# Layer-norm statistics on ScalarE for five tiles, one transposed buffer for two layers, and a new order of loads and matmuls in an MLP-mixer block

## The chip, the cores and the metric

One core of a Trainium2 chip runs the kernel. The metric is the device time of one execution in microseconds. Its engines: PE (TensorE, the matmuls), DVE (VectorE), ACT (ScalarE), POOL (GpSimd), SP (SyncE, which here only issues DMAs). "PEld" is PE's loading of weights, which overlaps its matmuls.

## The reference

x has 2048 rows of 512 in bf16; w1 and w2 are 512x512, w3 is 512x1792, w4 is 1792x512.

```python
def _layernorm(x, axis=-1, eps=1e-5):
    m = jnp.mean(x, axis=axis, keepdims=True)
    v = jnp.var(x, axis=axis, keepdims=True)
    return (x - m) / jnp.sqrt(v + eps)

def reference(x, w1, w2, w3, w4):
    B, S, D = x.shape
    h = _gelu(_layernorm(x, axis=-1) @ w1)
    c = D // 4
    g0 = jnp.pad(h[:, :, 0*c:1*c], ((0, 0), (1, 0), (0, 0)))[:, :S, :]
    g1 = jnp.pad(h[:, :, 1*c:2*c], ((0, 0), (0, 1), (0, 0)))[:, 1:, :]
    g2 = jnp.pad(h[:, :, 2*c:3*c], ((0, 0), (2, 0), (0, 0)))[:, :S, :]
    g3 = jnp.pad(h[:, :, 3*c:   ], ((0, 0), (0, 2), (0, 0)))[:, 2:, :]
    hs = jnp.concatenate([g0, g1, g2, g3], axis=-1) @ w2
    x1 = x + hs
    h2 = _gelu(_layernorm(x1, axis=-1) @ w3) @ w4
    return x1 + h2
```

## The kernel before

The rows are cut into 16 tiles of 128. Tile t of layer 1 has the number q = t, of layer 2 the number q = 16 + t. All weights and all of x stay in SBUF; each is read once.

**Stages.** `ln` (L272) makes statistics and normalized rows of a tile: bn_stats (L275, "bnst"), bn_aggr (L277, "bnag"), then the inverse root. For tiles 0 and 1 that is a square root on ACT (L281) and a reciprocal on DVE (L283); for the rest variance plus epsilon on DVE (L287, "vpe") and a power of -0.5 on POOL (L290, "rstd"). The rows are normalized on DVE (L296), ACT (L304) or POOL (L307), by the table `NORM`; ACT and POOL also need "nmr" (L300), minus mean times rstd, from DVE. Matmuls need the tile transposed: by four PE transposes (`pe_transpose`, L316; matmul on L327, eviction on ACT L334 or DVE L337, by the table `EVAC`) for the tiles that the script names with `tp` or `ty` (they differ in the PSUM buffer), by a DMA transpose on SP (L313, "tp") for the rest.

`mm_up` (L341) multiplies the transposed rows of a group of tiles by w1 or w3 (L355), 128 output features at a time, and gelu on ACT (L370) evicts PSUM. `GROUPS` gives the tiles per group; a group of n tiles has matmuls of 128n columns. `mm_mix` (L379) multiplies the four shifted quarters of gelu's output by w2 for one tile (L395, four matmuls of 512 columns); shifts of one and two rows mean that it needs its neighbours' groups too. DVE adds x (L401, "x1"), and `ln(2, t)` follows. `mm_down` (L406) multiplies by w4 (L419, 14 matmuls of 512 columns, the last tile in two halves); DVE adds x1 (L427) and SP writes the tile out.

PSUM has three pairs of banks (`next_pair`) for up groups and `ty` transposes, and two single banks (`next_bank`) for mix, down and `tp` transposes; each is used in turn, so a step waits until the eviction of the step that held it last.

**Order.** PE follows `SCRIPT` exactly. A planner in `Program.order` (L48) lays out the other engines ahead of time: each operation has a cost and a due time counted back from PE's order, and the earliest due of the ready ones goes next. Every engine then runs its list strictly in that order, with semaphore waits where an operation needs another engine's result. An engine whose next operation isn't ready stands still, whatever is ready behind it. The loads go ahead of everything on SP. Twelve matmuls on zeros (L443) warm PE up. Two activations on a constant (L450, L452) bring in the tables for square root and gelu.

SP's order of loads before: x tiles 0, 1, 2, 3 (one each), w1 in two halves, x tiles 4-5, 6-7, w2, w3, x tiles 8-11, 12-15, w4 in two halves; then DMA transposes and writes.

The orders that the planner makes, of ACT and of PE, up to PE's first large stretch:

```
ACT  warm_sqrt sqrt1 sqrt0 warm_gelu ev1 ev0 ev2 gelu1_1 gelu1_0 gelu1_2 norm4 gelu1_3 norm7 ev4 ev6 gelu1_4 gelu1_5 gelu2_0 ...
PE   warm tp1 tp0 up1_1 tp2 up1_0 tp3 up1_2 mix0 tp5 up1_3 mix1 tp4 mix2 tp7 tp6 up1_4 up1_5 tp16 tp17 mix3 mix4 up2_0 ...
```

("up1_4" is group 4 of layer 1, "gelu1_4" its gelu, "ev" the eviction of a PE transpose.)

Of the kernel before, what the change touches and what calls it, by code (L numbers as in the profile page):

```python
# [6 lines left out]
P = 128  # L7
# [18 lines left out]
class Program:  # L26
# [17 lines left out]
    def line(self, names):  # L44

        self.lines.append(names.split())

    def order(self):  # L48
# [24 lines left out]
        named = {op.name: op for op in self.ops}  # L73
        for names in self.lines:
            for a, b in zip(names, names[1:]):
                assert named[a].eng == named[b].eng, (a, b)
                preds[named[b].idx].add(named[a].idx)
        last = None
        pe_pos = 0
        for op in self.ops:  # L80
            if op.eng == "pe":
                if last is not None:
                    preds[op.idx].add(last.idx)
                last = op
                op.prio = pe_pos
                pe_pos += 1
        succs = [set() for _ in self.ops]
# [41 lines left out]
        for op in self.ops:  # L129
            if op.first is not None:  # L130
                op.prio = op.first

# [8 lines left out]
        qfree = 0.0  # L141
        out = []
        while len(out) < len(self.ops):
# [12 lines left out]
            if op.queue is None:  # L156
                done = free[e] = start + op.dur
            else:
                free[e] = start + (1300.0 if op.queue == "tp" else (1000.0 if e == "pool" else 460.0))
                if op.queue == "tp":  # L160
                    done = max(start + 2300.0, qfree + 1200.0)
                else:
                    qfree = max(qfree, start + 1500.0) + op.dur
                    done = qfree + 350.0
            out.append(op)
            for j in succs[op.idx]:
# [3 lines left out]
                ready[j] = max(ready[j], done + hop)  # L170
                if npend[j] == 0:
                    cands[o.eng].append(o)
        self.seq = out
        self.total = max(free.values())
        return out

GROUPS = {1: (1, 1, 1, 1, 2, 2, 4, 4), 2: (2, 2, 4, 4, 4)}
NORM = {0: "pool", 4: "act", 5: "pool", 6: "pool", 7: "act", 8: "pool", 9: "pool", 10: "act", 11: "act", 16: "pool", 19: "pool", 20: "act", 21: "act"}
EVAC = {3: "dve", 5: "dve", 7: "dve", 16: "dve", 17: "dve"}
SCRIPT = """  # L180
warm:3 warm:9 ty:1 ty:0 up1:1 tp:2 up1:0 tp:3 up1:2 mix:0 ty:5 up1:3 mix:1 ty:4 mix:2 ty:7 ty:6 up1:4-5
ty:16-17 mix:3-4 up2:0 mix:5 up2:1 down:0 mix:6 up1:6 down:3 mix:7 mix:9-10 up1:7 mix:8 down:1 mix:14 up2:2
mix:15 mix:13 mix:11 down:7 down:2 down:6 down:5 mix:12 up2:3 down:4 down:11 down:10 up2:4 down:8 down:14
down:12 down:9 down:13 down:15
"""

def bass_standalone__mixer_s_mlp__prompt_kernel(nc, x, w1, w2, w3, w4, out):
# [5 lines left out]
    NHEAD = 2  # L193
    NXN, NO, NPAIR, NOB = 12, 4, 3, 2
    SHIFT = (1, -1, 2, -2)
    HTW = S + 4
    group_of = {(l, t): g for l in (1, 2) for g, (t0, n) in enumerate(groups[l]) for t in range(t0, t0 + n)}
# [4 lines left out]
    with ExitStack() as es:  # L202
# [4 lines left out]
        x1nT = sb("x1nT", [P, DC, S], BF16)  # L207
# [14 lines left out]
        sdv = sb("sdv", [P, NHEAD], F32)  # L222
# [10 lines left out]
        npair, nbank = [0], [0]  # L233
# [9 lines left out]
        def y_res(p):  # L243
            return [("y", p)]
# [16 lines left out]
        def load_x(eng, t0, n, after=()):  # L261
            return pg.add(eng, f"x_dma{t0}", lambda e: e.dma_start(x_sb[:, t0 : t0 + n, :], xt[:, t0 : t0 + n, :]),  # L262
                   reads=list(after), writes=[(("x", t), 0) for t in range(t0, t0 + n)], dur=n * 400.0, queue=eng)

        def load_w(eng, name, dst, src, c0, c1, after=()):
            return pg.add(eng, f"dma_{name}{c0}",
                   lambda e: e.dma_start(dst[:, c0:c1, :], src.rearrange("(c p) f -> p c f", p=P)[:, c0:c1, :]),  # L267
                   reads=list(after), writes=[((name, c), 0) for c in range(c0, c1)],
                   dur=(c1 - c0) * P * src.shape[1] * 2 / 330.0, queue=eng)


        def ln(layer, t):  # L272
            q = t if layer == 1 else NT + t
            src, rs = (x_sb[:, t, :], ("x", t)) if layer == 1 else (x1_sb[:, t, :], ("x1", t))
            pg.add("dve", f"bnst{q}", lambda e: e.bn_stats(st6[:, q, :], src),  # L275
                   reads=[(rs, 0)], writes=[(("st6", q), 0)], dur=605)
            pg.add("dve", f"bnag{q}", lambda e: e.bn_aggr(mv[:, q, :], st6[:, q, :]),  # L277
                   reads=[(("st6", q), 0)], writes=[(("mv", q), 0)], dur=75)
            if q < NHEAD:
                pg.add("act", f"sqrt{q}",  # L280
                       lambda e: e.activation(sdv[:, q : q + 1], mv[:, q, 1:2], ACT_F.Sqrt, bias=eps_c[:], scale=1.0),  # L281
                       reads=[(("mv", q), 0), (("eps",), 0), (("warm",), 0)], writes=[(("sdv", q), 0)], dur=190)
                pg.add("dve", f"rcp{q}", lambda e: e.reciprocal(rstd[:, q : q + 1], sdv[:, q : q + 1]),  # L283
                       reads=[(("sdv", q), 0)], writes=[(("rstd", q), 0)], dur=75)
            else:
                pg.add("dve", f"vpe{q}",
                       lambda e: e.tensor_scalar(vpe[:, q : q + 1], mv[:, q, 1:2], LN_EPS, None, ALU.add),  # L287
                       reads=[(("mv", q), 0)], writes=[(("vpe", q), 0)], dur=70)
                pg.add("pool", f"rstd{q}",
                       lambda e: e.tensor_tensor(rstd[:, q : q + 1], vpe[:, q : q + 1], neghalf[:], ALU.pow),  # L290
                       reads=[(("vpe", q), 0), (("neghalf",), 0)], writes=[(("rstd", q), 0)], dur=470)
            how = NORM.get(q, "dve")
            dst = xn_buf[:, q % NXN, :]
            if how == "dve":
                pg.add("dve", f"norm{q}",
                       lambda e: e.tensor_scalar(dst, src, mv[:, q, 0:1], rstd[:, q : q + 1], ALU.subtract, ALU.mult),  # L296
                       reads=[(rs, 0), (("mv", q), 0), (("rstd", q), 0)], writes=[(("xn", q % NXN), q)], dur=330)
            else:
# [7 lines left out]
                else:  # L306
                    f = lambda e: e.tensor_scalar(dst, src, rstd[:, q : q + 1], nmr[:, q : q + 1], ALU.mult, ALU.add)  # L307
                pg.add(how, f"norm{q}", f, reads=[(rs, 0), (("nmr", q), 0), (("rstd", q), 0)],
                       writes=[(("xn", q % NXN), q)], dur=710 if how == "act" else 760)
            if q not in pe_tp:  # L310
                xT = xnT if layer == 1 else x1nT
                pg.add("sp", f"tp{q}",
                       lambda e: e.dma_start(xT[:, :, P * t : P * (t + 1)], xn_buf[:, q % NXN, :], transpose=True),  # L313
                       reads=[(("xn", q % NXN), q)], writes=[(("xT", layer, t), 0)], queue="tp")

        def pe_transpose(t, q, pair):  # L316
            layer = 1 if q < NT else 2
            if pair:
                b, v = next_pair()
                dst, res = y_bf[:, b, 0:D], ("y", b)  # L320
            else:
                b, v = next_bank()
                dst, res = o_bf[:, b, 0:D], ("o", b)

            def f(e):
                for c in range(DC):
                    ins = e.transpose(dst[:, P * c : P * (c + 1)], xn_buf[:, q % NXN, P * c : P * (c + 1)], ident[:])  # L327
                return ins

            pg.add("pe", f"tp{q}", f, reads=[(("xn", q % NXN), q), (("ident",), 1)], writes=[(res, v)], dur=225)  # L330
            to = (xnT if layer == 1 else x1nT)[:, :, P * t : P * (t + 1)]
            frm = dst.rearrange("p (c s) -> p c s", c=DC)
            if EVAC.get(q, "act") == "act":
                pg.add("act", f"ev{q}", lambda e: e.activation(to, frm, ACT_F.Copy),  # L334
                       reads=[(res, v)], writes=[(("xT", layer, t), 0)], dur=480)
            else:
                pg.add("dve", f"ev{q}", lambda e: e.tensor_copy(to, frm),  # L337
                       reads=[(res, v)], writes=[(("xT", layer, t), 0)], dur=335)


        def mm_up(layer, g):  # L341
# [4 lines left out]
            wsb, wn, src = (w1_sb, "w1", xnT) if layer == 1 else (w3_sb, "w3", x1nT)  # L346
            for f0 in range(0, nfc, per):
# [3 lines left out]
                def f(e, p=p, f0=f0, k=k):  # L351
                    for i in range(k):
# [7 lines left out]
                       reads=[((wn, c), 0) for c in range(DC)] + [(("xT", layer, t), 0) for t in range(t0, t0 + n)],  # L360
# [18 lines left out]
        def mm_mix(t):  # L379
# [12 lines left out]
            def f(e):  # L392
                for j, s in enumerate(SHIFT):
# [6 lines left out]
            pg.add("dve", f"x1_{t}",  # L400
                   lambda e: e.tensor_tensor(x1_sb[:, t, :], dst, x_sb[:, t, :], ALU.add),  # L401
                   reads=[(("o", b), v), (("x", t), 0)], writes=[(("x1", t), 0)], dur=600)
# [3 lines left out]
        def mm_down(t):  # L406
# [3 lines left out]
            halves = 2 if last else 1  # L410
            W = D // halves
            for hh in range(halves):
                b, v = next_bank()
                dst = o_ps[:, b, 0:W]
                cs = slice(W * hh, W * (hh + 1))

                def f(e, dst=dst, cs=cs):
                    for fc in range(FC):
# [12 lines left out]
                       reads=[(("osb", oi, hh), t)], dur=400, queue="sp")  # L431
# [6 lines left out]
        def warm_pe(n):  # L438
            b, v = next_bank()

            def f(e):
                for _ in range(n):
# [7 lines left out]
        pg.add("act", "warm_sqrt", lambda e: e.activation(warm[:], eps_c[:], ACT_F.Sqrt),  # L450
               reads=[(("eps",), 0)], writes=[(("warm",), 0)], dur=1400)
        pg.add("act", "warm_gelu", lambda e: e.activation(warm[:], eps_c[:], ACT_F.Gelu_apprx_tanh),  # L452
               reads=[(("eps",), 0)] + [(("sdv", q), 0) for q in range(NHEAD)], writes=[(("warm",), 1)], dur=1400)
        loads = [load_x("sp", t, 1) for t in range(4)]
        loads += [load_w("sp", "w1", w1_sb, w1, 0, 2), load_w("sp", "w1", w1_sb, w1, 2, 4), load_x("sp", 4, 2),
                  load_x("sp", 6, 2), load_w("sp", "w2", w2_sb, w2, 0, DC), load_w("sp", "w3", w3_sb, w3, 0, DC),
                  load_x("sp", 8, 4), load_x("sp", 12, 4), load_w("sp", "w4", w4_sb, w4, 0, 7),
                  load_w("sp", "w4", w4_sb, w4, 7, 14)]
        for i, op in enumerate(loads):
            op.first = i - 100  # L460
# [5 lines left out]
        pe_tp = {n for kind, n in steps if kind in ("tp", "ty")}  # L466
        for t in range(NT):
            ln(1, t)
        for kind, n in steps:
# [8 lines left out]
            else:  # L478
                for _ in mm_up(int(kind[2]), n):
                    pass  # L480
        pg.order()
# [105 lines left out]
```

## Time and profile before

| what | value |
|---|---|
| median of three runs | 139.92 us (139.44 to 139.97) |
| the profiled execution's own time | 140.05 us |
| its span, first to last instruction | 137.5 us |
| granted TensorE clock over the span | 1.00 |
| HBM read, written | 6.82 MB, 2.10 MB |
| first tile lands / first useful PE work | 2.9 us / 5.63 us |

Times in the profile count from the span's start. The page's first part gives each engine's busy time and its share of the span; a later part follows the chain of work that ended last, from the last instruction backwards. In rows of groups, the figures are total busy time, mean ns of one, and the idle time of the engine ahead of it with what ended it. In rows of the timeline they are the start, the length, the engine and line, the output and input, and in brackets the idle time ahead. A DMA's figure is the time from issue to landing. Matmuls are pipelined, and their ends are modelled: 16 matmuls of 128 columns show as 1.05 us, but the next block can follow their start after 0.86.

### The profile page before, as it was taken

The numbers are of one execution on the slowest core, as the hardware profiler recorded it, in microseconds if no ns is written. First come the engines' busy times: TensorE is split into PE (matmuls) and PEld (weight loads), VectorE is DVE, ScalarE is ACT, GpSimd is POOL, SyncE is SP. The second block draws the span as 40 slices with busy tenths as digits, with TensorE's granted clock in tenths as the row PEclk, the third lists the DMA queues.
The fourth block names the chain that finished last, engine by engine and source line by source line (L and its number), as shares of the span: only waits on it lengthen the run. The fifth ranks groups of instructions, "written<-read, shape, count | busy, mean of one in ns | idle before, by whom it ended". The sixth has DMA issues, their size and how long they took to land.

```text
span 137.5 us, 1926 instructions
## 1 busy us (share of the span) xinstructions
PE 132.0 (96%) x762; PEld 70.1 (51%) x762; DVE 60.1 (44%) x167; ACT 47.5 (35%) x56; POOL 22.4 (16%) x47
## 2 busy tenths in 40 slices
PE   6689999999999999999999999999999999999992
PEld 2276777878444344444434444444444444444471
DVE  2979899997170798710097327100222000122231
ACT  4655652585623041255500001555100555200000
POOL 2246353675110014100004001000000000000000
DMA  4999996515454101530001521100011000011121
GB/s 107 301 291 370 376 348 198 81 38 112 84 109 114 43 0 38 102 89 0 0 5 35 117 76 38 38 0 0 5 38 58 18 0 0 0 38 43 46 68 38
DMA packets 20023, 11.91 MB, mean 87 GB/s; under 512 B 12464, under 2 KB 19504, under 8 KB 20016
## 3 DMA queue, kind: packets, MB, share of 16 engines
q1 hardware_dynamic: 20016, 11.80, 30.9%
q8 instruction: 6, 0.10, 0.3%
q14 instruction: 1, 0.01, 0.0%
HBM read 6.82 MB, written 2.10 MB: 65 GB/s over the span
## 4 chain that ended last, share of the span: by engine, by line
PE 90%; DMA 5%; SPq 3%; issue 0%; DVE 0%
PE y_ps L355 43%; PE o_ps L419 35%; PE o_ps L395 10%; DMA w_sb<-in_w_dram 5%; SPq L262 2%; PE y_ps L327 1%; SPq L267 1%; DVE o_sb L427 0%
## 5 line engine op out<-in xcount | busy, mean ns | idle before, releaser
L419 PE MATMUL o_ps<-w_sb,h2T 128*128 128x512 bf16 (+1 forms) x238 | 49.4, 366 | 0.0
L355 PE MATMUL y_ps<-x1nT,w_sb 128*128 128x512 bf16 (+1 forms) x280 | 49.3, 336 | 0.0
L370 ACT ACTIVATE h2T<-y_ps 128x1024 bf16<-128x1024 f32 (+1 forms) x29 | 28.6, 994 | 50.6 <-PE y_ps L355 50.6
L355 PEld LDWEIGHTS y_ps<-x1nT,w_sb 128*128 128x128 bf16 x280 | 27.4, 98 | 21.5
L419 PEld LDWEIGHTS o_ps<-w_sb,h2T 128*128 128x128 bf16 x238 | 23.2, 98 | 25.2 <-DVE x_sb L401 0.3
L427 DVE TENSOR_TENSOR o_sb<-o_ps,x_sb 128x512 bf16<-128x512 f32 (+1 forms) x17 | 11.2, 660 | 53.9 <-PE o_ps L419 50.9
L290 POOL TENSOR_TENSOR rstd<-vpe,neghalf 128x1 f32<-128x1 f32 x30 | 16.3, 556 | 57.1 <-DVE vpe L287 57.1
L275 DVE BATCH_NORM_STATS2 st<-x_sb 128x6 f32<-128x512 bf16 x32 | 21.7, 687 | 2.6 <-DMA x_sb<-in_x_dram 2.4
L401 DVE TENSOR_TENSOR x_sb<-o_ps,x_sb 128x512 bf16<-128x512 f32 x16 | 11.0, 689 | 12.4 <-PE o_ps L395 12.3
L395 PE MATMUL o_ps<-w_sb,hT 128*128 128x512 bf16 x64 | 15.8, 380 | 0.3 <-DMA w_sb<-in_w_dram 0.3
L355 PE MATMUL y_ps<-xnT,w_sb 128*128 128x128 bf16 (+2 forms) x128 | 15.1, 272 | 0.0
L370 ACT ACTIVATE hT<-y_ps 128x1024 bf16<-128x1024 f32 (+1 forms) x10 | 8.4, 854 | 14.4 <-PE y_ps L355 14.4
L355 PEld LDWEIGHTS y_ps<-xnT,w_sb 128*128 128x128 bf16 x128 | 9.9, 98 | 4.2
L395 PEld LDWEIGHTS o_ps<-w_sb,hT 128*128 128x128 bf16 x64 | 5.8, 98 | 7.3 <-DVE x_sb L401 0.7
L296 DVE TENSOR_SCALAR xn_buf<-x_sb,mv,rstd 128x512 bf16<-128x512 bf16 x19 | 7.6, 409 | 3.2 <-POOL rstd L290 2.6
L307 POOL TENSOR_SCALAR xn_buf<-x_sb,rstd,nmr 128x512 bf16<-128x512 bf16 x7 | 5.4, 772 | 5.9 <-DVE mv L277 5.1
L443 PE MATMUL o_ps<-zeros 128*128 128x512 bf16 x12 | 4.1, 509 | 1.2 <-DVE zeros L248 1.2
L277 DVE BATCH_NORM_AGGREGATE mv<-st 128x2 f32<-128x6 f32 x32 | 4.7, 170 | 0.3
L304 ACT ACTIVATE xn_buf<-x_sb,nmr,rstd 128x512 bf16<-128x512 bf16 x6 | 4.6, 810 | 0.3 <-DVE nmr L300 0.3
L287 DVE TENSOR_SCALAR vpe<-mv 128x1 f32<-128x1 f32 x30 | 3.8, 148 | 0.5
L327 PE MATMUL y_ps<-ident,xn_buf 128*128 128x128 bf16 x32 | 2.8, 220 | 1.1 <-POOL xn_buf L307 0.7
L327 PEld LDWEIGHTS y_ps<-ident,xn_buf 128*128 128x128 bf16 x32 | 2.1, 98 | 2.5 <-DVE xn_buf L296 0.9
(26 smaller groups left out, 15.6 us busy)
## 6 DMA issues: line engine op xcount, KB each, us to landing
out_dram<-o_sb SPq DMA_DIRECT2D x15, 128.0 KB, 1.7
w_sb<-in_w_dram SPq DMA_DIRECT2D x1, 1792.0 KB, 10.7
w_sb<-in_w_dram SPq DMA_DIRECT2D x2, 896.0 KB, 13.0
x_sb<-in_x_dram SPq DMA_DIRECT2D x2, 512.0 KB, 12.3
x_sb<-in_x_dram SPq DMA_DIRECT2D x4, 128.0 KB, 2.4
w_sb<-in_w_dram SPq DMA_DIRECT2D x2, 256.0 KB, 3.4
x_sb<-in_x_dram SPq DMA_DIRECT2D x2, 256.0 KB, 4.2
w_sb<-in_w_dram SPq DMA_DIRECT2D x1, 512.0 KB, 6.7
```

The lines of the kernel that those rows point to most:

```text
L275: pg.add("dve", f"bnst{q}", lambda e: e.bn_stats(st6[:, q, :], src), reads=[(rs, 0)], writes=[(("st6", q), 0)], dur=605)
L277: pg.add("dve", f"bnag{q}", lambda e: e.bn_aggr(mv[:, q, :], st6[:, q, :]), reads=[(("st6", q), 0)], writes=[(("mv", q), 0)], dur=75)
L290: lambda e: e.tensor_tensor(rstd[:, q : q + 1], vpe[:, q : q + 1], neghalf[:], ALU.pow),
L296: lambda e: e.tensor_scalar(dst, src, mv[:, q, 0:1], rstd[:, q : q + 1], ALU.subtract, ALU.mult),
L307: f = lambda e: e.tensor_scalar(dst, src, rstd[:, q : q + 1], nmr[:, q : q + 1], ALU.mult, ALU.add)
L327: ins = e.transpose(dst[:, P * c : P * (c + 1)], xn_buf[:, q % NXN, P * c : P * (c + 1)], ident[:])
L355: ins = e.matmul(y_ps[:, p, W * i : W * (i + 1)], wsb[:, dc, P * fc : P * (fc + 1)], src[:, dc, P * t0 : P * t0 + W], start=(dc == 0), sto ...
L370: (lambda d, s: (lambda e: e.activation(d, s, ACT_F.Gelu_apprx_tanh)))(dst, ysrc),
L395: ins = e.matmul(dst, hT[:, j, c0 : c0 + P], w2_sb[:, j, :], start=(j == 0), stop=(j == DC - 1))
L401: lambda e: e.tensor_tensor(x1_sb[:, t, :], dst, x_sb[:, t, :], ALU.add),
L419: ins = e.matmul(dst, h2T[:, fc, P * t : P * (t + 1)], w4_sb[:, fc, cs], start=(fc == 0), stop=(fc == FC - 1))
L427: (lambda d, c: (lambda e: e.tensor_tensor(o_sb[:, oi, c], d, x1_sb[:, t, c], ALU.add)))(dst, cs),
```

## The change

The order in which the planner's tables and script send the work is replaced, and so are some ways of doing it:

- `STAT_ACT`: tiles 1, 3, 6, 16 and 23 get their statistics from ACT: an activation Copy with its accumulator as the sum (layer 1 only; in layer 2 DVE's addition of x accumulates the sum itself) and an activation Square with its accumulator as the sum of squares. Three small DVE operations (mean, msq, vpe) make the variance of them, in place of bn_stats, bn_aggr and vpe.
- `SQRT`: the square root on ACT for tile 0 alone; tile 1 goes by POOL's power.
- `HALF`: tile 0 is loaded in two halves of 256 columns, one issued by SP and one by ACT, with a bn_stats for each.
- `NORM`: on POOL tiles 2 and 6 (before seven tiles), on ACT 7, 8, 18, 19, 21 (before six), the rest on DVE.
- `GROUPS`: layer 1 has six groups of two tiles behind the four single tiles; the two groups of four are gone.
- one buffer `xnT` for the transposed rows of both layers; `xn_buf` has 16 slots for 12, eight to each layer.
- eight tiles are transposed on PE (32 transposes) for ten before (40): 0, 1, 2, 5, 3, 4, 16, 17. Tile 5's eviction is shared by ACT and DVE.
- `LOADS`: a new order of loads on SP, held by a chain (`line`), with the second half of w4 behind tile 19's transpose.

The order of the same queues after, as built (ACT, PE and SP):

```
ACT  dma_x0_1 warm_sqrt sum1 ssq1 sqrt0 warm_gelu ev0 ev1 sum3 ssq3 gelu1_0 gelu1_1 gelu1_2 ev5act sum6 ev3 ssq16 ssq6 gelu1_3 gelu1_4 ev16 norm7 gelu2_0 ...
PE   warm tp0 tp1 tp2 up1_0 up1_1 up1_2 tp5 mix0 tp3 tp4 mix1 up1_3 up1_4 mix2 tp16 tp17 mix4 up2_0 mix3 up1_5 up1_6 mix6 up1_7 mix8 mix5 up1_8 mix10 mix9 up1_9 mix12 mix7 up2_1 mix13 up2_2 ...
SP   x2 x1 x0_0 x4-5 w1b w1a x3 w2 x6-7 w3 x8-11 x12-15 w4b tp6 tp7 tp8 ... tp15 tp18 tp19 w4a tp20 tp22 tp21 tp23 ...
DVE  zeros bnst2 bnst0_1 bnst0_0 bnag2 mean1 vpe2 bnag0 msq1 vpe1 rcp0 norm0 nmr2 norm1 bnst5 bnag5 vpe5 ev2 bnst4 mean3 norm5 msq3 vpe3 bnag4 vpe4 norm3 norm4 ev5dve x1_0 ev4 ...
```

The diff, cut to its core (the planner's own costs for landings are changed too, and left out here):

```diff
-GROUPS = {1: (1, 1, 1, 1, 2, 2, 4, 4), 2: (2, 2, 4, 4, 4)}
-NORM = {0: "pool", 4: "act", 5: "pool", 6: "pool", 7: "act", 8: "pool", 9: "pool", 10: "act", 11: "act", 16: "pool", 19: "pool", 20: "act", 21: "act"}
-EVAC = {3: "dve", 5: "dve", 7: "dve", 16: "dve", 17: "dve"}
+GROUPS = {1: (1, 1, 1, 1, 2, 2, 2, 2, 2, 2), 2: (2, 2, 4, 4, 4)}
+NORM = {2: "pool", 6: "pool", 7: "act", 8: "act", 18: "act", 19: "act", 21: "act"}
+EVAC = {2: "dve", 4: "dve", 5: "both", 17: "dve"}
+SQRT = (0,)
+STAT_ACT = (1, 3, 6, 16, 23)
+HALF = (0,)
+TAIL = (256, 256)
+LOADS = """
+x2 x1 x0 x4-5 w1b w1a x3 w2 x6-7 w3 x8-11 x12-15 w4b tp19 w4a
+"""
 SCRIPT = """
-warm:3 warm:9 ty:1 ty:0 up1:1 tp:2 up1:0 tp:3 up1:2 mix:0 ty:5 up1:3 mix:1 ty:4 mix:2 ty:7 ty:6 up1:4-5
-ty:16-17 mix:3-4 up2:0 mix:5 up2:1 down:0 mix:6 up1:6 down:3 mix:7 mix:9-10 up1:7 mix:8 down:1 mix:14 up2:2
-mix:15 mix:13 mix:11 down:7 down:2 down:6 down:5 mix:12 up2:3 down:4 down:11 down:10 up2:4 down:8 down:14
-down:12 down:9 down:13 down:15
+warm:12 ty:0-1 tp:2 up1:0-2 ty:5 mix:0 ty:3-4 mix:1 up1:3-4 mix:2 ty:16-17 mix:4 up2:0 mix:3 up1:5-6 mix:6
+up1:7 mix:8 mix:5 up1:8 mix:10 mix:9 up1:9 mix:12 mix:7 up2:1 mix:13 up2:2 mix:11 down:0-1 mix:15 up2:3 mix:14
+down:3 down:2 down:5 up2:4 down:6 down:4 down:7-8 down:12 down:11 down:9 down:13 down:10 down:14-15
 """
...
-    NXN, NO, NPAIR, NOB = 12, 4, 3, 2
+    NXN, NO, NPAIR, NOB, NJ = 16, 4, 3, 2, 4
+    slot = lambda q: q % (NXN // 2) + (NXN // 2) * (q // NT)
-        x1nT = sb("x1nT", [P, DC, S], BF16)
...
+            if q in STAT_ACT:
+                if layer == 1:
+                    b, v = next_junk()
+                    pg.add("act", f"sum{q}",
+                           (lambda d: (lambda e: e.activation(d, src, ACT_F.Copy, accum_out=sums[:, q, 0:1])))(
+                               junk[:, b, :]),
+                           reads=rs, writes=[(("sum", q), 0), (("junk", b), v)], dur=610)
+                b, v = next_junk()
+                pg.add("act", f"ssq{q}",
+                       (lambda d: (lambda e: e.activation(d, src, ACT_F.Square, accum_out=sums[:, q, 1:2])))(
+                           junk[:, b, :]),
+                       reads=rs, writes=[(("ssq", q), 0), (("junk", b), v)], dur=610)
+                pg.add("dve", f"mean{q}",
+                       lambda e: e.tensor_scalar(mv[:, q, 0:1], sums[:, q, 0:1], 1.0 / D, None, ALU.mult),
+                       reads=[(("sum", q), 0)], writes=[(("mv", q), 0)], dur=75)
...
+            for eng, c0, c1 in (("act", 0, 2), ("dve", 2, 4)) if how == "both" else ((how, 0, DC),):
...
+            if NT + t in STAT_ACT:
+                f = lambda e: e.scalar_tensor_tensor(x1_sb[:, t, :], dst, 1.0, x_sb[:, t, :], ALU.mult, ALU.add,
+                                                     accum_out=sums[:, NT + t, 0:1])
...
+        pg.line(queue)
         pg.order()
```

## The prediction, made before the changed kernel was run

> **What bounds the kernel now.** I read the page's share of busy time first, then the chain of work that ended last, then the timeline of the first 25 us and PE's waits. From the page:
>
> ```profile
> PE 132.0 (96%) x762; PEld 70.1 (51%) x762; DVE 60.1 (44%) x167; ACT 47.5 (35%) x56; POOL 22.4 (16%) x47
> PE 90%; DMA 5%; SPq 3%; issue 0%; DVE 0%
> L443 PE MATMUL o_ps<-zeros 128*128 128x512 bf16 x12 | 4.1, 509 | 1.2 <-DVE zeros L248 1.2
> ```
>
> PE is the bound, and 4.1 us of its 132.0 are warm-up. The chain in order of time shows where PE's unbroken stretch begins and ends:
>
> ```profile
> 4.60 6.67 DMA w_sb<-in_w_dram
> 11.27 0.05 issue
> 11.31 1.04 PE o_ps L395 x4
> ...
> 116.84 18.18 PE o_ps L419 x98
> 135.02 0.02 issue
> 135.04 0.43 DVE o_sb L427
> ```
>
> Everything before 11.31 is the wait for w2, issued at 4.60 and landing 6.67 later; from there every piece is PE until 135.02. PE's waits after the warm-up add to 1.9 us, all before 11.31:
>
> ```profile
> PE y_ps L327 <- POOL xn_buf L307: 0.7, 1, 0.7
> PE o_ps L327 <- DVE xn_buf L296: 0.5, 1, 0.5
> PE y_ps L327 <- DVE xn_buf L296: 0.4, 1, 0.4
> PE o_ps L395 <- DMA w_sb<-in_w_dram: 0.3, 1, 0.3
> ```
>
> So a change can win only by starting the first mixing matmuls (mix0, L395) earlier, or by taking work out of PE. It can lose wherever a reordered tile isn't ready.
>
> **PE's work.** From the chain: four transposes of a tile 0.22 us, 16 matmuls of 128 columns 0.86, 16 of 256 columns 1.745 (3.49 for 32), 16 of 512 columns 3.45, one mix tile 0.86. The new order has 32 transposes for 40: -0.45. Layer-1 groups of four tiles become groups of two: four times 1.745 for two times 3.45, +0.08. Everything else on PE is only moved. Before mix0 stand the same four tile transposes and three 128-column groups in both. So behind mix0 PE has 0.37 us less to do, if no hole opens.
>
> **When mix0 can start: the weights.** The issues on SP come some 0.47 us apart, and landings follow the bytes ahead of them. Before, the timeline and DMA windows put 1.28 MB at 7.58 (tiles 4-5), 1.54 MB at 8.39 (tiles 6-7), 2.05 MB at 11.27 (w2). After, w2 has 1.79 MB up to its end, since tiles 6-7 go behind it: between 8.39 and 11.27, in a straight line 9.8. The last stretch before was slow, so I allow 9.8 to 10.6. w1 ends at 1.15 MB (about 7.0), tile 3 at 1.28 MB (7.58), tiles 6-7 at 2.05 MB (11.27, w2's old place). Half of tile 0 goes out on ScalarE's queue: one more issue of about 0.45 us ahead of the first table load, which still ends by 2.5, before x1 lands at about 3.45.
>
> **When mix0 can start: ScalarE.** These rows give the steps:
>
> ```profile
> 4.45 0.48 ACT L281 ACTIVATE sdv<-mv,eps_c 128x1 f32<-128x1 f32 x2 [2.24 <-DVE mv L277]
> 4.95 1.28 ACT L452 ACT_TABLE_LOAD   x1
> 6.25 0.20 ACT L452 ACTIVATE warm<-eps_c 128x1 f32<-128x1 f32 x1
> 6.36 0.58 ACT L334 ACTIVATE xnT<-y_ps 128x512 bf16<-128x512 bf16 x1
> 7.08 1.05 PE L355 MATMUL y_ps<-xnT,w_sb 128*128 128x128 bf16 x16
> 9.58 1.08 ACT L370 ACTIVATE hT<-y_ps 128x512 bf16<-128x512 f32 x2
> ```
>
> From a square root's end to the first eviction is 1.43 us, an eviction or gelu of 512 elements occupies 0.54, and PE follows an eviction by 0.14. The accumulating activations (sum, ssq; tiles 1, 3, 6, and ssq alone for 16, 23) are not in the trace. Nearest rows: the gelu at 0.54 and the normalization on ScalarE (L304) at 0.81, which reads two per-partition operands that these don't; reading out the accumulator may come on top. Bounds 0.60 to 1.05; I take 0.70, nearer the gelu, whose operand form they share.
>
> The Trainium skill (ScalarE: Activation LUTs, Rules for kernel authors) says to give additions and multiplications to VectorE, up to three times as fast per element in bf16. It speaks against this: one statistics instruction on DVE (L275, 687 ns, 0.61 apart) becomes two on ScalarE, 1.4 us. By engine time the five tiles lose some 3 us; by the trace it matters only where ScalarE is in front of PE, so I lay out that queue. The same page (What ACT_TABLE_LOAD costs) gives about 2.66 us for a switch of tables, drain included; this trace has 1.30 from the load to the next activation (4.95 to 6.25). By the rule the first eviction would be 1.4 us later than below; I take the row.
>
> With 0.70: sum1 3.48, ssq1 4.18 to 4.88 (DVE has tile 0's statistics by about 4.65), sqrt0 to 5.17, first eviction 6.60 to 7.18, first up group 7.32 (w1 is there at 7.0). Transposes 0, 1, 2 come at about 5.9, 6.3 and 6.9: norm0 follows sqrt0 by 0.23, PE a norm by 0.47; rstd1 waits behind rstd2 on POOL, 0.55 each, and tile 2's norm on POOL takes 0.77. Up groups 0 to 2 then run unbroken to 9.91, tile 5's transpose to 10.13. ScalarE: second eviction to 7.70, sum3 and ssq3 (tile 3 landed 7.58) to 9.10, gelu of tile 0 to 9.64, of tile 1 finished 10.24, mix0 at 10.37. The two limits, w2 at 9.8 to 10.6 and ScalarE at 10.37, meet: **mix0 at 10.4 for 11.31, -0.91.**
>
> **Behind mix0.** PE: mix0 to 11.26, transposes 3 and 4 to 11.71, mix1 to 12.57, then up group 3, which needs tile 3's eviction. On ScalarE that stands behind sum6, which waits for tiles 6-7 (11.27): 11.3 to 12.0, eviction to 12.59, PE 12.72. **A hole of 0.15** (none if the tiles land 0.15 earlier, 0.6 if 0.45 later); behind the waiting sum6 are also ssq16, ssq6 and gelu 3, needed only by mix2 at 15.3. Gelu 4 ends at 16.5 and mix4 comes at 16.64: no hole, no slack.
>
> Next, the transposes by DMA. Two more tiles go that way, and tp6 to tp19 stand on SP behind the first half of w4, with w4's other half behind them.
>
> ```profile
> 28.65 10.36 SPq L313 DMA_TRANSPOSE xnT<-xn_buf  x8
> x1nT<-xn_buf SPq DMA_TRANSPOSE x14, 2.5
> ```
>
> That is 1.3 us of SP for each and 2.5 to landing. norm6 on POOL ends at 18.75 (tile 16 and 17's evictions, nmr6 at 17.3, rstd7, then 0.77), so tp6 to tp11 issue at 18.8, 20.1, 21.4, 22.7, 24.0, 25.3. PE unbroken needs tiles 6-7 at 24.5 (tp7 lands 22.6), 8-9 at 26.2 (25.2), 10-11 at 28.8 (27.8), 12-13 at 32.3 (30.4), 14-15 at 35.8 (34.0), 18-19 at 39.2 (x1_5 at 33.1 on DVE, nmr19 34.1, norm19 35.0, tp19 at 35.5, landing 38.0). Margins of 1.0 to 1.9: covered, but this cover is new. Without it each us late is a us lost. w4's second half issues at about 37 and is needed near 60. The accumulating add on DVE (x1_0; nearest row L401, 0.69, bounds 0.69 to 1.0) is hidden behind tile 16's ssq, up to 0.5. DVE's 25 norms for 19, the shared transposed buffer (its readers finished long before) and the new buffer slots meet no wait that I find. The tail, two half tiles, is the same.
>
> **Sum**, against the profiled execution (span 137.5, time 140.05, 0.13 above the median): -0.91 - 0.37 + 0.15 = -1.13. Span 136.4; from the median, 139.92 - 1.13 = **138.8**.
>
> **Rivals.** *The head stays where it was (chance 0.24).* For it: two uncertain terms, activation price and w2's landing, each sets mix0. At 0.90 an activation, evictions and sum3 both move, mix0 = 7.51 + 4 x 0.90 = 11.1, and the hole grows to 0.3: -0.2 - 0.37 + 0.3, 139.65. Against: the gelu row at 0.54. Break-even needs about 1.0.
>
> *Transposes blocked behind loads (0.13): slower.* Before, no transpose was issued until 22.88, when the loads were nearly in. After, tp6 follows a load whose place in the queue took 5.17 us to issue from 7.22, as if the queue had no room. If tp6 gets through only when that load has landed (21.6), tp9 lands at 21.6 + 3.9 + 2.5 = 28.0 where PE wants 26.2: +1.8, so 140.6. It costs from an issue of tp6 at 19.8 on, and decides the sign at 20.9. Against: that load's issue ended at 12.39, 6 us before tp6.
>
> *The likeliest (0.63):* 138.2 to 139.2. Its low end is an activation at 0.60 and no hole: mix0 10.05, -1.26 - 0.37.
>
> A measurement of this kernel tells about 0.5% (0.7 us) from no change. Faster by more: 0.62 (the likeliest, less its upper edge); within: 0.25 (the first rival, and that edge); slower: 0.13. The range runs from 138.2 to 140.2; it leaves out most of the slow rival.
>
> **What would show it.** Right: mix0 starts near 10.4, with ScalarE's gelu as its releaser or w2 a few tenths off; sum activations 0.65 to 0.75 apart; a hole of a few tenths ahead of up group 3; none later. Wrong: mix0 near or past 11; an accumulator read of over 0.2 us as a row of its own; PE waiting on transposes at 24 to 40 us.

## The result, and the profile after

The changed kernel takes 138.49 us (median of six runs, 138.22 to 139.22) against 139.94 us: a ratio of 0.9902, 95% interval 0.9872 to 0.9931, so 1.45 us less. The forecast was 138.8, in sum nearly right. Its terms were not: the head of the kernel gained a quarter of what I had given it, and over two fifths of the gain lie outside the profile's span, where I had put nothing. (Ratios and medians leave out executions that were over 1.5% slower than the fastest of their kernel; the profiled ones of e4 and e6 were such, so no trace of theirs is read.)

The shares, and PE's waits after the change:

```profile
PE 131.7 (96%) x786; PEld 73.1 (53%) x786; DVE 58.8 (43%) x169; ACT 51.4 (38%) x70; POOL 19.5 (14%) x43
PE 92%; DMA 2%; DVE 1%; POOL 1%; SPq 1%; issue 0%; ACT 0%
PE o_ps L535 <- DVE zeros L269: 1.2, 1, 1.2
PE y_ps L415 <- DVE xn_buf L372: 1.0, 1, 1.0
PE o_ps L415 <- POOL xn_buf L383: 0.2, 1, 0.2
```

Behind the warm-up PE waits 1.2 us where it had waited 1.9, and no longer for w2. The chain of waits after (start, length, what) shows what took w2's place:

```profile
1.66 3.22 DMA x_sb<-in_x_dram
...
4.91 0.43 DVE st6b L343
...
5.75 0.30 ACT sdv L360
...
6.92 0.94 POOL xn_buf L383
...
7.91 0.40 PE o_ps L415 x4
8.30 2.73 PE y_ps L442 x48
11.04 0.22 PE y_ps L415 x4
11.26 0.86 PE o_ps L482 x4
...
134.22 0.02 issue
134.24 0.42 DVE o_sb L519
```

SP's half of tile 0 lands at 4.88; statistics, square root, tile 2's norm on POOL and its transpose follow (beside them, ScalarE's table load and first eviction end at about 8.05), and PE is unbroken from the first up group to the end. mix0 comes at 11.26 only because three up groups and a transpose stand ahead of it. (In the timeline by starts it is 11.10, against 11.31 before.) PE ends at 134.22 for 135.02.

The 1.45 us, by place. The median span fell from 137.5 to 136.65 (the profiled ones: 137.5, 136.7), 0.85. The rest is time less span: about 2.5 us in every run of the kernel before, 1.8 in every run after. Within the span, mix0's start gives 0.21 and the stretch behind it 0.59. Of that stretch I had counted 0.37. The other 0.2 I had overlooked: two stretches of three mix tiles in a row, which with two PSUM banks are longer than three times 0.86. In the chain before:

```profile
44.98 2.69 PE o_ps L395 x12
...
67.96 2.69 PE o_ps L395 x12
```

Each has 0.1 us in it that is not matmul: the third tile's bank is free only when DVE has added x to the first (PE's weight loads wait 0.3 and 0.4 us for it). After the change no three mix tiles follow each other.

### The profile page after: what moved, and what is told of

It reads as the page before. It is cut to its first block, busy times and chain, and to the rows that moved or that the text cites. A ratio compares the mean times of both kernels' runs of the same rounds, so it can differ in the third digit from the quotient of the medians.

```text
span 136.7 us, 1989 instructions
## 1 busy us (share of the span) xinstructions
PE 131.7 (96%) x786; PEld 73.1 (53%) x786; DVE 58.8 (43%) x169; ACT 51.4 (38%) x70; POOL 19.5 (14%) x43
## 4 chain that ended last, share of the span: by engine, by line
PE 92%; DMA 2%; DVE 1%; POOL 1%; SPq 1%; issue 0%; ACT 0%
PE y_ps L442 46%; PE o_ps L511 35%; PE o_ps L482 10%; DMA x_sb<-in_x_dram 2%; PE y_ps L415 1%; POOL xn_buf L383 1%; SPq L296 1%; DVE st6b L343 0%; DVE o_sb L519 0%; DVE xn_buf L372 0%; PE o_ps L415 0%; ACT sdv L360 0%; DVE mv L346 0%; DVE rstd L362 0%; DVE nmr L376 0%
## 5 line engine op out<-in xcount | busy, mean ns | idle before, releaser
L442 PE MATMUL y_ps<-xnT,w_sb 128*128 128x256 bf16 (+2 forms) x440 | 64.3, 305 | 0.0
L442 PEld LDWEIGHTS y_ps<-xnT,w_sb 128*128 128x128 bf16 x440 | 40.3, 98 | 23.8 <-ACT h2T L457 0.3
L511 PEld LDWEIGHTS o_ps<-w_sb,h2T 128*128 128x128 bf16 x238 | 23.3, 98 | 25.3
L366 POOL TENSOR_TENSOR rstd<-vpe,neghalf 128x1 f32<-128x1 f32 x31 | 17.0, 559 | 61.9 <-DVE vpe L355 49.9
L493 DVE TENSOR_TENSOR x_sb<-o_ps,x_sb 128x512 bf16<-128x512 f32 x14 | 9.6, 688 | 22.2 <-PE o_ps L482 22.2
L349 DVE BATCH_NORM_STATS2 st<-x_sb 128x6 f32<-128x512 bf16 x26 | 17.5, 685 | 2.4 <-DMA x_sb<-in_x_dram 2.2
L372 DVE TENSOR_SCALAR xn_buf<-x_sb,mv,rstd 128x512 bf16<-128x512 bf16 x25 | 10.2, 411 | 3.8 <-POOL rstd L366 2.8
L351 DVE BATCH_NORM_AGGREGATE mv<-st 128x2 f32<-128x6 f32 x26 | 4.1, 174 | 0.2
L535 PEld LDWEIGHTS o_ps<-zeros 128*128 128x128 bf16 x12 | 1.5, 135 | 3.7 <-issue 2.5
L324 ACT ACTIVATE junk<-x_sb 128x512 bf16<-128x512 bf16 x5 | 3.1, 630 | 0.7 <-DVE x_sb L489 0.7
L420 ACT ACTIVATE xnT<-y_ps 128x512 bf16<-128x512 bf16 (+1 forms) x5 | 2.6, 549 | 0.1
## 6 DMA issues: line engine op xcount, KB each, us to landing
x_sb<-in_x_dram SPq DMA_DIRECT2D x2, 512.0 KB, 10.8
```

Of the source, the lines that this page charges most:

```text
L366: lambda e: e.tensor_tensor(col(rstd), col(vpe), neghalf[:], ALU.pow),
L442: ins = e.matmul(y_ps[:, p, W * i : W * (i + 1)], wsb[:, dc, P * fc : P * (fc + 1)], src[:, dc, P * t0 : P * t0 + W], start=(dc == 0), sto ...
L493: f = lambda e: e.tensor_tensor(x1_sb[:, t, :], dst, x_sb[:, t, :], ALU.add)
L511: ins = e.matmul(dst, h2T[:, fc, P * t : P * (t + 1)], w4_sb[:, fc, cs], start=(fc == 0), stop=(fc == FC - 1))
L535: ins = e.matmul(o_ps[:, b, :], zeros[:, 0:P], zeros[:], start=True, stop=True)
```

## The experiments

Each edit is to the changed kernel unless it says otherwise. "Outside" is time less span, the median over a kernel's runs.

**e1: statistics all on DVE.**

```diff
-STAT_ACT = (1, 3, 6, 16, 23)
+STAT_ACT = ()
```

> All 32 tiles get bn_stats on DVE again (STAT_ACT empty), the rest as after the change. Theory 1, the head is set by tile 0 (its half from SP lands at 4.88 us, square root at 5.75, PE unbroken from 8.20): DVE has room for tile 1's statistics before that landing, so the square root does not move, PE's unbroken stretch still begins at 8.2 to 8.4, 138.5 to 138.8 us. Rival, ScalarE's accumulators carry the gain by taking work from DVE: five times 0.61 us more on DVE delays norms and evictions, PE's first holes grow by 0.6 us or more, 139.1 us or above.

Measured: 139.70 us, ratio to before 1.0011 (0.9977 to 1.0045): the whole gain is gone. The profiled span is 137.5, 0.8 above the change's; some 0.3 of the loss lies outside it (2.10 us for 1.83). Its chain:

```profile
4.66 0.75 DVE st6b L343 x2
...
6.03 0.60 DVE st L349
6.63 0.07 DVE rstd L362
6.73 0.41 DVE xn_buf L372
...
8.68 2.68 PE y_ps L442 x48
...
13.36 1.20 DVE x_sb L493 x2
14.55 1.19 DVE st L349 x2
...
16.09 1.08 POOL rstd L366 x2
...
17.68 0.38 PE y_ps L415 x4
```

The landing at 4.63 is no later, so theory 1 falls. DVE is in the chain twice: at 6.03, where a bn_stats of a tile not yet needed stands ahead of tile 0's reciprocal and norm, and from 13.36, where two additions and two bn_stats in a row make tiles 16 and 17 late. PE's unbroken stretch begins at 8.68 for 8.30 and has holes ahead of the transposes of 16 and 17. The rival holds: in this order of work ScalarE's accumulators earn their place by emptying DVE.

**e2 and e5: tile 0 whole, third or first on SP, nothing on ScalarE's queue.**

```diff
-HALF = (0,)
+HALF = ()
 # e5 also
-x2 x1 x0 x4-5 w1b w1a x3 w2 ...
+x0 x2 x1 x4-5 w1b w1a x3 w2 ...
```

> Tile 0 is loaded whole by SP, third in its order; nothing is issued by ScalarE's queue (HALF empty). Theory 1a, the second queue's transfer slows the first landings: tile 0 then lands near 4.15 us as the third tile did before, the square root comes at about 5.0 instead of 5.75, PE is unbroken from about 7.5, 137.8 us. Theory 1b, landing goes by bytes alone: the whole tile lands 0.2 to 0.3 us later than its half did, 138.7 to 138.9 us.

> As e2, but tile 0 is the first load of SP. Theory 1: tile 0 lands near 2.9 us, and the square root waits for ScalarE's two accumulations of tile 1 (lands near 4.15, done near 5.4): 0.35 us earlier than now, 138.1 us. If tile 0's landing did not set the head, no change: 138.5 us.

Measured: e2 138.81 us (0.9909; 0.9874 to 0.9945), e5 138.99 us (0.9927; 0.9900 to 0.9954); no gain in either, and neither interval parts from the change's own. In e2 tile 0 landed at 4.58, 0.3 earlier, and the wait only changes its name:

```profile
3.10 5.25 DMA w_sb<-in_w_dram
8.36 0.05 issue
8.40 2.85 PE y_ps L442 x48
```

The second half of w1 landed at 8.36; it had landed at 7.22 with the same bytes ahead of it in the change's trace. In e5 the head did come earlier, the up groups at 7.93 for 8.30, and the time was given back where DMA transposes came late. Chain of e5:

```profile
7.93 2.72 PE y_ps L442 x48
...
25.42 4.20 DMA xnT<-xn_buf
29.62 0.14 issue
29.76 1.91 PE y_ps L442 x16
```

That transpose took 4.2 us to land, for 2.5 in the median, and PE stood still 0.5 us ahead of up group 7 (another 0.2 near 47 us). DMA in e5 between 26.4 and 27.2 us:

```profile
q1 hardware_dynamic: 391, 0.10, 62.9%
q8 instruction: 1, 0.02, 11.8%
```

One packet of the instruction queue moves in that stretch. In the changed kernel such a packet went at 30.8 us, beside a transpose (issued at 30.66) that took 3.0 us, but PE did not wait for that tile. The coincidence is in all twelve traces read here: one such packet moves between 25 and 31 us, and a transpose issued 0.1 to 1.8 us before it takes 3.0 to 4.2 us. Whether that costs anything depends on how soon PE wants that tile. That the packet is the cause was not tested.

**e4, e6, e8: tile 2's norm on DVE (e4), more time for the transposes (e8), both (e6).**

```diff
 # e4, e6
-NORM = {2: "pool", 6: "pool", 7: "act", ...
+NORM = {6: "pool", 7: "act", ...
 # e6, e8
-... w4b tp19 w4a
+... w4b tp23 w4a
-up1:7 mix:8 mix:5 up1:8 mix:10 ...
+mix:5 up1:7 mix:8 up1:8 mix:10 ...
```

> Tile 2 is normalized on DVE, not on POOL, whose 0.94 us stands in the chain of waits after the change. If that step alone holds PE, tile 2's transpose comes 0.3 us earlier and so does the end: 138.2 us. If the first eviction on ScalarE is just as late (square root 5.75, table load to 7.35, eviction to 8.05, PE 8.18 against 8.20 now), nothing is gained: 138.5 us.

> The change with only the two moves of e6 that give the DMA transposes time, tile 2's norm left on POOL. Theory: no hole stood there in the profiled run, so its median stays at 138.5 us, but runs as slow as 139.2 us go. Rival: mix5 earlier makes its own wait for a bank of PSUM, 138.7 us or more.

> e4 (tile 2's norm on DVE) with more time for the DMA transposes: mix5 goes ahead of up group 7, which gives tiles 10 and 11 0.86 us more, and w4's second half goes behind tile 23's transpose. Theory, e4's holes of 1.4 and 1.3 us are transposes that land late and find only 1 us of slack: both holes close or shrink to 0.6 us, 138.2 to 138.6 us with the spread of e4's runs (138.6 to 141.4) gone. Rival, the holes come from norms that are late on DVE and POOL whatever the order: still 139.5 us or more.

Measured: e4 139.65 us (0.9969; 0.9932 to 1.0005), worse than both of its expectations; e6 139.23 us (0.9940; 0.9917 to 0.9962); e8 138.43 us (0.9894; 0.9866 to 0.9921), its runs from 138.33 to 138.79. e8 is as fast as the change; six runs cannot tell it from it. e6 is 0.4 us below e4, but their intervals overlap; that thin slack is a part of e4's loss is not shown. What the room is for can be seen in e8's trace: the sixth transpose (tile 11's in the change's order), issued at 25.77, took 4.04 us and landed at 29.81, later than the 29.4 at which PE reached its group in the change; with mix5 ahead PE came at 30.16 and did not wait. The 0.8 us that e6 stays above e8 is not explained: the two differ in tile 2's norm and in the order that the planner then makes on DVE.

**e3: all tables of before in the changed code.** What stays are the shared buffer, the 16 slots and the planner's own changes (new costs of landings and transposes, another handling of the order of loads).

```diff
-(GROUPS, NORM, EVAC, SCRIPT, LOADS of the change; SQRT = (0,), STAT_ACT = (1, 3, 6, 16, 23), HALF = (0,))
+(those of before; SQRT = (0, 1), STAT_ACT = (), HALF = ())
```

> The changed code with all tables of before (groups, norms, evictions, script, loads, two square roots, no accumulators, tile 0 whole): what stays of the change is the one transposed buffer, the 16 buffer slots and the planner's new costs. Theory 1, the gain lies in the tables: span 137.5 us and 139.9 us as before, with mix0 waiting for w2 near 11.3 and the two holes of 0.08 us. Rival, the code itself carries the part of the gain that lies outside the span (time less span was 2.5 us before, 1.8 us after): same span, 139.2 us.

Measured: 139.44 us, 0.9958 (0.9937 to 0.9979), between both expectations. The span's median is 137.05, outside 2.4. So about a third of the gain (0.5 us; the interval allows 0.3 to 0.9) comes without any new table. In the order that the new planner makes, tile 2's norm stands ahead of tile 5's bn_stats on DVE (before, behind it). PE then no longer waits for that norm, as the lines of before showed, but for w1:

```profile
PE y_ps L443 <- DMA w_sb<-in_w_dram: 0.8, 1, 0.8
PE y_ps L416 <- POOL xn_buf L384: 0.7, 1, 0.7
```

In this trace PE ends at 134.83, 0.2 earlier than before, where the span's median fell by 0.45, so the reordering is not shown to be the whole of e3's gain.

**e7: the old order of loads.**

```diff
-HALF = (0,)
+HALF = ()
-x2 x1 x0 x4-5 w1b w1a x3 w2 x6-7 w3 x8-11 x12-15 w4b tp19 w4a
+x0 x1 x2 x3 w1a w1b x4-5 x6-7 w2 w3 x8-11 x12-15 w4a w4b
```

> After the change, with the load order of before (x tiles 0 to 3, w1, tiles 4-5, 6-7, w2, w3, the rest of x, both halves of w4, then the transposes) and tile 0 whole. Theory from the prediction, w2's place sets mix0: w2 lands near 11.3 again, mix0 is 0.1 to 0.3 us later, and tile 6 is earlier; about 138.8 us. Rival, the order of loads beyond the first tiles carries the gain, since both halves of w4 now keep the first transposes waiting to 20 us or later: holes at up group 5 to 7, 139.5 us or more.

Measured: 139.19 us, 0.9948 (0.9921 to 0.9975), 0.7 above the change. Neither reason that I gave is in its trace: PE's only waits behind the warm-up are these, and the transposes make no hole.

```profile
PE y_ps L415 <- DVE xn_buf L372: 1.2, 2, 0.9
...
PE o_ps L482 <- issue: 0.2, 1, 0.2
```

The first row's two waits are for norms on DVE. In this trace the order of loads acts through what it lets DVE do first: tiles 6-7 land earlier (9.42 for 10.00), and the planner puts a bn_stats of theirs ahead of the norms of tiles 3 and 4. That accounts for PE's end, 0.35 us later than in the change; the rest of the 0.7 is not traced.

**e10: tiles 0, 1, 2 whole and in order, on e8.**

```diff
-HALF = (0,)
+HALF = ()
-x2 x1 x0 x4-5 w1b ...
+x0 x1 x2 x4-5 w1b ...
```

> e8 (the change, with more time for the DMA transposes) with tiles 0, 1, 2 loaded whole by SP in this order and nothing on ScalarE's queue. Theory, the half on the second queue delays tile 0 (4.65 to 4.93 us against 3.7 to 4.6 for a whole tile in third place) and so the head: tile 0 at 2.9, tile 1 at 3.3, square root at about 5.0, PE unbroken from 7.5 unless w1 (7.0 to 8.4) holds it: 137.7 to 138.1 us. Rival, the landing of w1 takes the place of tile 0's: 138.4 us, as e8.

Measured: 139.54 us, 0.9975 (0.9949 to 1.0001), slower than e8 by 1.1. Tile 0 lands at 2.8 and the first transpose starts at 5.86, but the chain then goes through w2:

```profile
4.11 6.69 DMA w_sb<-in_w_dram
...
11.07 0.81 PE o_ps L482 x3
...
45.09 2.49 DMA xnT<-xn_buf
```

mix0 waits some 0.3 us for w2, which landed at 10.8. (The record of its first matmul is missing, so that it seems to start at 11.07; the transposes behind it start at 11.72, for 11.96 in the change.) So little of the earlier tile 0 is left. A second hole of 0.9 us stands ahead of 47.7: tile 23's transpose, issued 2.3 us later than in e8 (42.82).

**e11: two tiles more on PE, on e8.**

```diff
-up2:0 mix:3 up1:5-6
+up2:0 mix:3 ty:6-7 up1:5-6
```

> e8 with tiles 6 and 7 transposed on PE again (ten tiles, 40 transposes), ahead of up group 5. If PE's work is the bound there, the eight transposes cost 0.45 us: 138.9 us. If the two evictions on ScalarE make PE wait too, 139.4 us or more. Rival, two DMA transposes fewer free SP and close a hole: 138.4 us or less.

Measured: 139.86 us, 0.9991 (0.9967 to 1.0015), 1.43 above e8. Beside 0.45 of matmuls, PE waits for the evictions:

```profile
PE y_ps L442 <- ACT xnT L420: 1.0, 1, 1.0
```

So a tile transposed by DMA, where it has the time, is worth more than its 0.22 us of PE.

**e9 and e12: what lies outside the span.** e9 is the kernel before with layer-1 groups of two; e12 is e8 with five norms moved to POOL at places with time to spare.

```diff
 # e9, on the kernel before
-GROUPS = {1: (1, 1, 1, 1, 2, 2, 4, 4), ...
+GROUPS = {1: (1, 1, 1, 1, 2, 2, 2, 2, 2, 2), ...
-... up1:6 down:3 ... up1:7 mix:8 ...
+... up1:6-7 down:3 ... up1:8-9 mix:8 ...
 # e12, on e8
-NORM = {2: "pool", 6: "pool", ..., 21: "act"}
+NORM = {2: "pool", 6: "pool", ..., 21: "act", 24: "pool", 25: "pool", 26: "pool", 28: "pool", 29: "pool"}
```

> The kernel before, with one part of the change alone: the two layer-1 groups of four tiles become four groups of two, at the same places in PE's order. PE has 32 matmuls more and 0.08 us more work: 140.0 us, span 137.6. Theory A, the time outside the span goes with the number of PE's instructions (2.5 us with 762 matmuls, 1.8 with 786): it falls to about 1.8 us here, 139.4 us. Theory B, it goes with something else: it stays at 2.5 us.

> e8 with the norms of tiles 24, 25, 26, 28 and 29 on POOL, seven norms there as before the change, at places where the transposes have time to spare. Theory A, the time outside the span (2.5 us before and in the kernels with seven norms on POOL, 1.8 to 2.1 us with one or two) goes with POOL's work: span 136.6 as e8, time 139.1 us. Theory B, it goes with something else: 138.4 us, 1.8 us outside. A hole in PE near 48 to 80 us would show that the norms had no time to spare; then the span grows.

Measured: e9 140.38 us, 1.0022 (0.9996 to 1.0048), with 2.47 us outside; the number of PE's instructions is not it. e12 138.88 us, 0.9908 (0.9879 to 0.9937), with the same profiled span as e8 (e8's rows first, then e12's):

```profile
span 136.6 us, 1976 instructions
PE 130.9 (96%) x773; PEld 73.1 (54%) x786; DVE 58.8 (43%) x169; ACT 51.3 (38%) x70; POOL 19.3 (14%) x43
...
span 136.6 us, 1981 instructions
PE 131.3 (96%) x773; PEld 73.2 (54%) x786; DVE 57.6 (42%) x169; ACT 51.3 (38%) x70; POOL 23.0 (17%) x48
```

POOL has 48 instructions for 43, PE ends at the same time, and outside there are 2.43 us for e8's 1.82. Theory A holds in so far as norms moved from DVE to POOL cost time that the span does not show, here 0.6 us for five. Each such norm also brings a small operation on DVE ("nmr": 7 in e8, 12 in e12, 13 before), and the two were not separated. It is no simple count: outside is 2.4 to 2.5 with seven norms on POOL (before, e3, e9, e12), 1.8 to 2.0 with one or two (the change, e2, e4 to e8, e10, e11), but 2.1 in e1 with two. What happens there, no view shows.

## Why the prediction was right, and where it was not

**PE's work, -0.37: right**, and 0.2 too small, since I took each mix stretch as 0.86 a tile and not from its own row (2.69 for three).

**mix0 at 10.4, -0.91: wrong; -0.21.** It started at 11.10: "near or past 11" was my own sign of being wrong. The step that failed is tile 0's statistics "by about 4.65". They were ready at 5.73, since SP's half of the tile landed only at 4.88; from landing to statistics the trace has 0.85, so my 4.65 would have needed a landing near 3.8. The third load of SP, a whole tile, landed between 3.8 and 4.6 in the traces of before, e2, e3, e5, e7, e9 and e10 (4.17 before). With the other half on ScalarE's queue, SP's half landed between 4.6 and 4.9 in the change, e1, e8, e11 and e12. The square root came at 5.75 for my 4.88, and the first up group at 8.20 (its start) for 7.32; 0.7 of that 0.9 is left at mix0. Neither of the two limits that I had let meet at 10.4 set it: w2 landed at 9.29 (and w1 at 7.22, which is where my own rows put 1.15 MB, not at 7.0), the gelu of tile 1 ended at 10.77, and PE itself came at 11.10. So the head stayed nearly where it was, as in my first rival, but not by that rival's causes. The accumulating activations cost 0.61, of which the read-out, a row of its own of 0.19 to 0.21, is hidden but for 0.09 (my 0.70; low bound 0.60). Timeline after:

```profile
3.54 0.63 ACT L319 ACTIVATE junk<-x_sb 128x512 bf16<-128x512 bf16 x1 [0.91 <-DMA x_sb<-in_x_dram]
...
4.08 0.19 ACT L319 ACTIVATION_READ_ACCUMULATOR junk<-x_sb 128x1 f32 x1
...
4.17 0.62 ACT L324 ACTIVATE junk<-x_sb 128x512 bf16<-128x512 bf16 x1
```

Nor would a better guess for tile 0 have made 10.4 true of a kernel: e2, e5 and e10 remove that wait, and w1 (8.36 in e2), w2 (10.8 in e10) or tile 1 with its two accumulations (landed 4.12 in e5) takes its place. At the same place in the queue, the second half of w1 landed between 7.0 and 8.4 and w2 between 9.3 and 10.8 in the traces with the new order of loads.

**The table switch**: 1.29 us from the load's start to the next activation (6.07 to 7.36). The row of before, not the 2.66 of the Trainium skill (ScalarE: Activation LUTs, What ACT_TABLE_LOAD costs), was the one to take.

**ScalarE against VectorE.** I weighed the Trainium skill's rule (ScalarE: Activation LUTs, Rules for kernel authors) as a cost of ScalarE's time and left out what DVE gains. e1 shows what the change loses without it: 1.2 us in all. By the rule those instructions belong on VectorE; measured, that is slower here, since in e1 DVE stands in the chain of waits at two places.

**The hole of 0.15 ahead of up group 3: absent.** Tiles 6-7 landed at 10.0, not 11.27.

**The DMA transposes: right up to tile 19.** tp6 to tp11 were issued from 19.3 to 25.9 (predicted 18.8 to 25.3), tp11 landed at 28.4, PE reached up group 7 at 29.4: the 1.0 us of slack that I gave it. (At that spacing tp15 would land at 33.0, not at my 34.0; it landed at 35.1, and PE came at 36.4.) The slow rival cost nothing, but its mechanism is in the traces, on the landing and not on the issue: in all twelve, the first transpose issued while a weight load was in flight landed 0.5 to 1.8 us after that load, and none before it. In the change w4's first load landed at 21.34, so tp6, issued at 19.32, came no later than usual (21.81); in e7 w4's last half landed at 24.12 and tp6 took 5.2 us. I had not looked beyond tile 19, at the transposes behind w4's other half (issued at 37.39, landed at 42.84). In the change the next three took 5.2, 4.4 and 3.7 us, and the fourth, tile 23's, landed at 46.67, only 0.14 before PE's group at 46.81. The load is not all of it: in e8, where it goes behind tile 23, three transposes issued from 40.05 on still took 4.6, 3.7 and 3.0 us, beside an instruction packet at 42.5. Up group 7 was the right place to watch: e5 lost 0.5 us there.

**Time outside the span: not in the sum at all.** I took the 2.55 us of the profiled run as fixed. It fell by 0.7, and e12 ties that to norms taken off POOL. Without that, the change would have been some 139.2 us, 0.5% better and no more. That the sum came near was luck: -0.7 here and -0.2 in the mix stretches stood in for the -0.7 missing at mix0, and there was no hole of 0.15.

**Open**: the 0.8 us between e6 and e8; whether the instruction packet delays the transposes; why norms moved to POOL cost time outside the span, and why e1 has 2.1 there.

## What to carry to other kernels

Cost work that is moved from one engine to another on both: the engine that loses it may be the one in front of the bound, and in this kernel taking that part out again (e1) cost 1.2 us, all that the change had gained. The parts do not add up: tile 2's norm put back on DVE (e4) cost as much. Where several loads feed the start, removing the one in the chain uncovers the next; list the landings of all of them before giving a gain to one. Where transposes follow a load on the same queue, count their landing from the load's. Compare time less span between versions before the span's change is taken for the gain.

## What the runs showed that I had not expected

- 0.6 us of device time outside the profiled span for five norms of 128x512 moved from DVE to POOL, with the span unchanged (e12 against e8).
- The first DMA transpose issued while a weight load was still in flight landed 0.5 to 1.8 us after that load, in each of the twelve traces; the median of all transposes was 2.5 us from issue to landing.
- A 64 KB half of a tile on SP, beside a half issued by ScalarE, took 3.0 to 3.2 us to land; a whole 128 KB tile at the same place in the queue took 2.1 to 2.6, in e2 2.9. The first tile of SP also landed at 3.2 to 3.3 us beside that second queue, at 2.8 to 3.0 without it.
- On DVE the read-out of an accumulator behind an addition from PSUM took 0.08 us, on ScalarE 0.19 to 0.21 us, the latter mostly hidden.
